# A gated feed-forward kernel: the joint stage starts at unit 3, with the x transposes and raw products of the second pass rearranged

## The chip, the cores and the metric

The kernel runs on one core of one Trainium2 chip. The metric is the device time of one execution in microseconds (us). Every time below comes from timed runs or from one profiled execution, whose trace counts from its own first instruction.

## The reference

The inputs are bfloat16: x is 2048 x 1024, w_gate and w_up are 1024 x 3584, w_down is 3584 x 1024.

```python
g = jnp.einsum("bsd,df->bsf", x, w_gate)
u = jnp.einsum("bsd,df->bsf", x, w_up)
h = gelu_tanh(g) * u
return jnp.einsum("bsf,fd->bsd", h, w_down)
```

## The kernel before

**Tiling.** The 3584 columns of the gate and up weights are cut into 14 *units* of 256. The 2048 rows of x are cut into two *passes* of 1024, each of two halves c = 0 and 1 with 512 rows. For one unit and one pass, weights (two blocks of 128 columns by two halves of the 1024 contracted elements) and x (two halves of the contraction by two halves of the rows) form a 2 x 2 by 2 x 2 block product, and the kernel forms it with seven products where the plain way takes eight. A product is four matmuls of 128 x 128 by 128 x 512, for gate and for up, so a unit and a pass take 56 matmuls. Two of the seven, the *raw products* (`raw_first`, `raw_second`, lines 229 to 236), take bfloat16 weights and x as they are. The five others take sums in float32: `s1` to `s4` of the weights (`sums_s`, line 173; `sa` is a cast), `t1` to `t4` of x (`sums_t`, line 149; `tb` is a cast).

**The separate stage.** Unit 0 of pass 0 is done in the plain way. After that `items` (line 911) lists seven pairs (unit, pass), each run by `unit` (line 252): (1,0), (2,0), (3,0), (2,1), (3,1), (1,1), (0,1). The order within `unit` is: s2·t2, s1·t1, s3·t3, s4·tb, then `whole_p4` (line 286), which calls `ahead` (raw products of later items), multiplies sa·t4 and calls `behind`. `unit` calls `aside(-2)`, `aside(-1)`, `aside(0)` and `aside(1)` at marked points, and `after_p5` behind s1·t1; there loads, transposes and GpSimd's sums are issued. Each item stores four blocks of h to DRAM (`times`, line 217).

**The joint stage.** From unit `JOINT = 4` on, a unit is done for both passes together (`joint_ops`, line 348), in an order written out by hand: `SEQUENCE_FIRST` for the first joint unit, `SEQUENCE` for the others. Here the two passes and the gate and up halves form a second 2 x 2 scheme (`inner`, line 380): seven products of two matmuls, 14, where the two passes apart take 16. It is used for s4·tb ("X") and sa·t4 ("K") in every joint unit, and for s3·t3 ("H") from unit `DIVIDED7 = 5` on. A unit of both passes takes 112 matmuls apart, 108 with X and K, 106 with all three. The inner scheme needs more sums on GpSimd: `split_b` (line 296) makes twelve 128 x 512 blocks for tb and t4 once, `split_b_rest` four more, `split_sums` (line 201) four 128 x 256 blocks for each unit and product.

**Queues.** Instructions of SyncE (which issues all DMAs), VectorE, GpSimd and TensorE go out in program order, ScalarE's too in this stage. x reaches its transposed form with DMA transposes (`transposing`, line 802), each 512 rows by 128 columns. Eight of them (pass 0, c = 1) are followed by unit 2's weights (line 827). Pass 1 needs sixteen: `XT[1, 0]` lies in `xT[1]`, `XT[1, 1]` in a tile "h01" (`late_half`, line 84) whose room t4 of pass 1 takes over later. They are issued in four groups of four (line 1071). Unit 3's weights are loaded ahead of the first group (line 1026). GpSimd makes s1 to s4 of units 2, 3, 0 and 4 and t1 to t4 of pass 1 in `at_p5` (line 925). Most tiles come from a pool of 58 slots of 2 KB in each partition; `wpool` holds two weight tiles of 8 KB.

The last stage, `down` (line 692), multiplies h with w_down in the same manner.

Of the kernel before, what the change touches and what calls it, by code (L numbers as in the profile page):

```python
# [10 lines left out]
def kernel(  # L11
# [10 lines left out]
    nc = tc.nc  # L22
# [15 lines left out]
    NKB = Dm // P  # L38
# [5 lines left out]
    NPASS = S // (2 * N)  # L44
    NU = NFB // 2
    NWARM = 7
    JOINT = 4
    DIVIDED7 = 5
    STAY = range(11, 14)
    KEEPS = [(u, n) for u in range(JOINT + 1, NU) for n in range({7: 2, 9: 2, 11: 2, 13: 3}.get(u, 1))]  # L50
    H, Q, R2 = NJ // 2, N // 2, range(2)
    SLOTS = 58
    STAGED = 3
# [27 lines left out]
    def staged():  # L81
        return opool.tile([P, N], bf16, name="o", tag="o")

    def late_half(p):
        if p:
            tile = hpool.tile([P, NJ, N], bf16, name="h01")
            XT[p, 1] = [tile[:, k] for k in range(NKB)]
        else:
            tiles = [slot([P, 2, N], bf16, "x") for _ in range(KH)]
            XT[p, 1] = [tiles[k // 2][:, k % 2] for k in range(NKB)]  # L90
# [37 lines left out]
    def load_w(u, slots=False):  # L128
        f0 = u * 2 * P
        if slots:  # L130
            w = [[slot([P, KH, 2 * P], bf16, "w") for _ in range(2)] for _ in range(2)]
        else:
            tile = wpool.tile([P, 2, NKB, 2 * P], bf16, name="w")
            w = parts(tile)
        for i, src in enumerate((w_gate, w_up)):
            src = src[:, f0 : f0 + 2 * P].rearrange("(ko ki) f -> ki ko f", ki=P)
            if slots:
                for half in range(2):
                    nc.sync.dma_start(out=w[i][half], in_=src[:, half * KH : (half + 1) * KH])
            else:  # L140
                nc.sync.dma_start(out=tile[:, i], in_=src)
        return w
# [6 lines left out]
    def sums_t(p, eng, place):  # L149
        K = range(KH)  # L150
        lo, hi = [[XT[p, c][k0 : k0 + KH] for c in range(2)] for k0 in (0, KH)]

        def put(name, k, a, b):
            t = place(name)
            eng(t, a, b, SUB)
            return t

        def put_cast(name, a):
            t = place(name)
            nc.scalar.copy(out=t, in_=a)  # L160
            return t

        return Sums(
            how={
                "t1": lambda q: [put("t1", k, lo[1][k], lo[0][k]) for k in K],
                "t2": lambda q: [put("t2", k, hi[1][k], q["t1"][k]) for k in K],
                "t3": lambda q, K=K: [put("t3", k, hi[1][k], lo[1][k]) for k in K],
                "t4": lambda q: [put("t4", k, hi[0][k], q["t2"][k]) for k in K],
                "tb": lambda q: [put_cast("tb", hi[1][k]) for k in K],
            }  # L170
        )
# [653 lines left out]
    for ko in range(NKB):  # L825
        transposing(0, 1, ko)
    ahead = load_w(2, True)

    def plain(ps, c, kos, parts=1):
        n = N // parts  # L830
# [51 lines left out]
            finish(bank[4:8], 1)  # L882
            t["t3"] = t3 + t["how"]["t3"](t, range(2, KH))

    spots = {}

    def new_room(kh, c, *names):
        tile = hpool.tile([P, H, N], f32r, name=f"h{kh}{c}")
        for i, name in enumerate(names):
            spots.setdefault(name, []).append(tile[:, i])  # L890

    new_room(0, 0, *["tb"] * KH, *["n"] * 3)
    new_room(1, 0, *["t2"] * KH, *["t1"] * 3)
    new_room(1, 1, "t1", *["t3"] * KH, *["n"] * 2)

    def place1(name):
        return spots[name].pop(0)

    def more_room():
        extra = wpool.tile([P, KH, N], f32r, name="w")  # L900
        spots["n"] += [extra[:, k] for k in range(KH)]

    def place_n():
        return spots["n"].pop(0)

    Ea, Eb, K, D = even, dd, cc, odd
    ws = {1: w, 2: ahead}
    ss = {1: s}
    sums, ns = {}, {}
    pairs = [[(2, 0), (3, 0)], [(2, 1), (3, 1)], [(1, 1), (0, 1)]]  # L910
    items = [(1, 0)] + [item for pair in pairs for item in pair]

    def loaded(u):
        return ws[u]

    def new_s(u, *names):
        if u not in ss:
            ss[u] = sums_s(loaded(u), pool)
        ss[u].make(*names)

    def raw_of(u, p, e, c):
        p1 = raw_products(e, c, p, loaded(u))
        return lambda: finish_raw(u, p, c, p1)

    def at_p5(n):
        u, p = items[n]
        if n == 0:
            pool_behind(t["t4"][-1])
            new_s(2, "s1", "s2", "s3", "s4")
        elif n == 1:  # L930
            new_s(3, "s1", "s2", "s3", "s4")
        elif n == 2:
            T[1] = sums_t(1, pool, place1)
            T[1].make("t1", "t2", "t3", "tb")
            new_room(0, 1, *["t4"] * KH, *["n"] * 3)
            T[1].make("t4")
        elif n == 3:
            new_s(0, "s1", "s2")
        elif n == 4:
            new_s(0, "s3", "s4")  # L940
            split_b("tb")
        elif n == 5:
            new_s(JOINT, "s1", "s2", "s3", "s4")
        elif n == 6:
            more_room()
            split_b("t4")

    keeps = {}
    for j, (u, n) in zip([*range(NJ)], KEEPS):
# [72 lines left out]
        if not more:  # L1022
            last_loads(what)

    turns = [(c, ko) for ko in range(NKB) for c in (1, 0)]
    loads = {(0, 0): [3], (4, 1): [JOINT]}

    def last_loads(what):
        for n in {"start": range(4, 6), "store": range(6, 10), "t4.0": range(10, 13), "s1": range(13, NJ)}.get(what, ()):
# [22 lines left out]
    with tc.manual_schedule(engines={ENG.Activation}):  # L1052
        for n, (u, p) in enumerate(items):
            first = n == 0
            m = (n - 1) // 2
            b = n % 2 == 0
            follow = pairs[m + 1] if m + 1 < len(pairs) else None

            def after_p5():
                at_p5(n)  # L1060

            def aside(part):
                if first and part < 0:
                    rest_of_0(part + 2)
                if first and part == 0:
                    t.make("t4")
                for v in loads.get((n, part), ()):
                    ws[v] = load_w(v, v == 0)
                if (n, part) == (0, 0):
                    late_half(1)  # L1070
                if (n, part) in ((0, 0), (0, 1), (1, 0), (1, 1)):
                    for c, ko in turns[:4]:
                        transposing(1, c, ko)
                    del turns[:4]

            def mid():
                if "sa" not in ss[u]:
                    ss[u]["sa"] = sums_s(loaded(u), pool)["how"]["sa"](None)

            def ahead_of_p4():  # L1080
                if b and follow:
                    raw_of(*follow[0], Ea, D)()
                    nxt["c11"] = raw_of(*follow[1], K, D)

            def behind_p4():
                if n == 2:
                    ws[0] = load_w(0, True)
                if "c11" in nxt:
                    nxt.pop("c11")()

            def after_first():
                raw_of(2, 0, even, cc)()
                nxt["c11"] = raw_of(3, 0, dd, cc)

            def p4(c12):
                times(p, 2 * u, 1, gelu(c12[0]), c12[1])
                if first:
                    whole_p4(u, p, odd, ss[u], after_first, behind_p4)
                else:
                    if n == len(items) - 1:  # L1100
                        split_b_rest("tb")
                        half_sums(JOINT, "tb", 0), half_sums(JOINT, "tb", 1)
                    whole_p4(u, p, (Ea, Eb)[b], ss[u], ahead_of_p4, behind_p4)
                    if n == len(items) - 1:
                        split_b_rest("t4")

            if first:
                banks = odd, cc, dd
                late = lambda: add(cc, nxt["p1"])
            else:  # L1110
                banks = (Eb, D, K) if b else (Ea, K, D)
                late = None
            unit(u, p, banks, ss[u], late, after_p5, aside, mid, p4)
            ss[u].pop("sa")
            if b and not first and follow:
                Ea, Eb, K, D = Ea, K, D, Eb

        E, F = [Ea, D], [K, Eb]
        last = None
        for u in range(JOINT, NU):  # L1120
            now = joint_ops(u, E, F)
            steps = SEQUENCE_FIRST if u == JOINT else SEQUENCE
            for name in steps:
                if name[0] == "@":
                    side_work(u, name[1:])
                elif name[0] != "-":
                    now[name]()
                elif last:
                    last[name]()
            last = now  # L1130
            E, F = F, E
        for name in SEQUENCE:
            if name[0] == "-":
                last[name]()
# [51 lines left out]
```

## Time and profile before

| | |
|---|---|
| median of three runs | 527.5 us (527.44 to 528.07) |
| the profiled execution's own time | 528.0 us |
| its span, first to last instruction | 526.2 us |
| TensorE (PE) busy | 521.6 us, 99% of the span, 2393 matmuls |
| VectorE (DVE) busy | 386.0 us, 73% |
| GpSimd (POOL) busy | 332.3 us, 63%; 8 tenths or more of every slice from 39 to 342 us |
| ScalarE (ACT) busy | 291.4 us, 55% |
| granted TensorE clock | 1.000 |

The timelines quoted below give the start in us, the duration in us, engine (SPq is SyncE's queue of DMA issues), line, operation, what is written and read, and the count of a merged group. Matmuls overlap in the records, so the pitch of a group is read from one group's start to the next one's.

### The profile page before, as it was taken

The numbers are of one execution on the slowest core, as the hardware profiler recorded it, in microseconds if no ns is written. First come the engines' busy times: TensorE is split into PE (matmuls) and PEld (weight loads), VectorE is DVE, ScalarE is ACT, GpSimd is POOL, SyncE is SP. The second block draws the span as 40 slices with busy tenths as digits, with TensorE's granted clock in tenths as the row PEclk, the third lists the DMA queues.
The fourth block names the chain that finished last, engine by engine and source line by source line (L and its number), as shares of the span: only waits on it lengthen the run. The fifth ranks groups of instructions, "written<-read, shape, count | busy, mean of one in ns | idle before, by whom it ended". The sixth has DMA issues, their size and how long they took to land.

```text
span 526.2 us, 7935 instructions
## 1 busy us (share of the span) xinstructions
PE 521.6 (99%) x2393; PEld 369.4 (70%) x2393; DVE 386.0 (73%) x588; ACT 291.4 (55%) x535; POOL 332.3 (63%) x339
## 2 busy tenths in 40 slices
PE   8999999999999999999999999999999999999997
PEld 5568686877667676767676676754788884488887
DVE  2984546337888889898989889896879326967934
ACT  2555755656777687868787786851135601143430
POOL 1169989988999999999999999940000000000694
PEclk9999999999999999999999999999999999999999
DMA  9685334131625357363727454999987999992732
GB/s 248 139 212 124 100 109 117 44 110 46 206 87 184 111 190 225 113 203 133 248 92 229 149 171 153 318 374 407 389 267 237 394 388 364 387 323 99 241 133 67
DMA packets 105194, 106.96 MB, mean 203 GB/s; under 512 B 19776, under 2 KB 83264, under 8 KB 105152
## 3 DMA queue, kind: packets, MB, share of 16 engines
q1 hardware_dynamic: 105152, 106.46, 62.3%
q8 instruction: 19, 0.31, 0.3%
q14 instruction: 23, 0.19, 0.1%
HBM read 73.66 MB, written 29.62 MB: 196 GB/s over the span
## 4 chain that ended last, share of the span: by engine, by line
PE 98%; DMA 1%; SPq 0%; DVE 0%; issue 0%
PE bank L120 98%; DMA w<-in_w_up_dram 1%; SPq L790 0%; SPq L810 0%; DVE st L99 0%
## 5 line engine op out<-in xcount | busy, mean ns | idle before, releaser
L120 PE MATMUL bank<-h,s 128*128 128x512 f32 x492 | 129.1, 394 | 0.0
L102 POOL TENSOR_TENSOR q<-q 128x256 fp32r<-128x256 f32 x28 | 27.0, 994 | 143.7 <-DMA q<-td 143.1
L120 PE MATMUL bank<-xT,w 128*128 128x512 bf16 (+1 forms) x472 | 107.8, 376 | 0.1
L120 PEld LDWEIGHTS bank<-h,s 128*128 128x128 f32 x492 | 92.4, 188 | 20.6
L120 PEld LDWEIGHTS <-w 128*128 128x128 bf16 x504 | 45.8, 98 | 59.0 <-issue 10.0
L102 POOL TENSOR_TENSOR s<-w 128x512 fp32r<-128x512 bf16 (+1 forms) x74 | 76.0, 1040 | 13.9 <-DMA w<-in_w_gate_dram 12.5
L120 PE MATMUL bank<-t,s 128*128 128x512 f32 x276 | 75.3, 399 | 0.0
L120 PE MATMUL bank<-q 128*128 128x512 f32 x264 | 65.6, 390 | 0.0
L120 PEld LDWEIGHTS bank<-t,s 128*128 128x128 f32 x276 | 51.9, 188 | 12.0
L116 ACT COPY p<-bank 128x512 f32<-128x512 f32 x76 | 42.9, 588 | 28.1 <-PE bank L120 28.1
L120 PEld LDWEIGHTS bank<-q 128*128 128x128 f32 x264 | 49.6, 188 | 10.4
L99 DVE TENSOR_TENSOR q<-h,h 128x512 fp32r<-128x512 bf16 x56 | 38.4, 686 | 17.1 <-DMA h<-hd 17.1
L116 ACT COPY u<-bank 128x512 f32<-128x512 f32 x62 | 35.9, 589 | 24.1 <-PE bank L120 21.5
L102 POOL TENSOR_TENSOR s<-s,s 128x256 fp32r<-128x256 f32 x57 | 42.7, 770 | 1.5
L120 PEld LDWEIGHTS <-h 128*128 128x128 bf16 x224 | 21.7, 98 | 26.5 <-issue 0.5
L102 POOL TENSOR_TENSOR s<-w,s 128x512 fp32r<-128x512 bf16 (+1 forms) x36 | 38.6, 1086 | 0.0
L99 DVE TENSOR_TENSOR xz<-bank,xz 128x512 f32<-128x512 f32 x40 | 27.6, 692 | 14.9 <-PE bank L120 8.1
L111 ACT CAST tb<-raw 128x512 fp32r<-128x512 bf16 x28 | 17.0, 631 | 36.7 <-DMA raw<-in_w_down_dram 26.1
L102 POOL TENSOR_TENSOR s<-s,w 128x512 fp32r<-128x512 f32 (+1 forms) x36 | 36.6, 1031 | 0.8
L102 POOL TENSOR_TENSOR m<-raw,m 128x512 fp32r<-128x512 bf16 x28 | 34.5, 1234 | 2.2
L99 DVE TENSOR_TENSOR bank<-bank,u 128x512 f32<-128x512 f32 x47 | 32.4, 688 | 0.0
L99 DVE TENSOR_TENSOR sum<-bank,p 128x512 f32<-128x512 f32 x14 | 9.7, 690 | 27.0 <-PE bank L120 23.1
(122 smaller groups left out, 929.6 us busy)
## 6 DMA issues: line engine op xcount, KB each, us to landing
raw<-in_w_down_dram SPq DMA_DIRECT2D x68, 256.0 KB, 3.8
q<-td SPq DMA_DIRECT2D x66, 256.0 KB, 5.4
td<-m SPq DMA_DIRECT2D x42, 256.0 KB, 2.6
hd<-o SPq DMA_DIRECT2D x72, 128.0 KB, 1.7
h<-hd SPq DMA_DIRECT2D x17, 512.0 KB, 6.9
hd<-h SPq DMA_DIRECT2D x38, 128.0 KB, 1.9
h<-hd SPq DMA_DIRECT2D x5, 768.0 KB, 8.2
out_dram<-st SPq DMA_DIRECT2D x30, 128.0 KB, 4.4
```

The source lines that it names most:

```text
L99: nc.vector.tensor_tensor(out=out, in0=a, in1=b, op=op)
L102: nc.gpsimd.tensor_tensor(out=out, in0=a, in1=b, op=op)
L111: nc.scalar.copy(out=t, in_=src)
L116: nc.scalar.copy(out=t, in_=ps)
L120: nc.tensor.matmul(ps, lhsT=lhs, rhs=rhs, start=start, stop=stop, skip_group_check=True)
```

## The change

Three things change together.

1. `JOINT` becomes 3. The items become (1,0), (2,0), (2,1), (1,1), (0,1). Unit 3 is the first joint unit (`SEQUENCE_FIRST`), unit 4 runs in `SEQUENCE`, with H still whole. Unit 3's weights go to slots and are loaded in the third item, unit 0's are not loaded again but read from the first tile. GpSimd's work is rearranged: t1 to t4 of pass 1 as eight instructions of 128 x 1024 instead of sixteen of 128 x 512, and earlier; the split of t4 after the last item has begun.
2. The sixteen transposes of pass 1 are issued in groups of 4, 4, 2, 2, 2, 2, the first behind unit 2's weights (before any store of h), the others at the points `aside(-2)`, `(-1)`, `(0)`, `(1)` of item (1,0) and `aside(-2)` of item (2,0). Their order is now: the lower half of the contraction for both c, then the upper half for c = 1, then the upper half for c = 0.
3. The raw products of (3,0) vanish from item (1,0). In item (2,0) the raw products of pass 1 are ordered: `raw_first` of unit 2, `raw_first` of unit 1, `raw_second` of unit 2, then sa·t4, then `raw_second` of unit 1 into the same banks.

```diff
-    JOINT = 4
+    JOINT = 3
+    AHEAD = {(0, -2): 4, (0, -1): 2, (0, 0): 2, (0, 1): 2, (1, -2): 2}
...
     ahead = load_w(2, True)
+    late_half(1)
+    turns = [(c, ko) for ko in range(KH) for c in (1, 0)] + [(c, ko) for c in (1, 0) for ko in range(KH, NKB)]
+
+    def turn_some(n):
+        for c, ko in turns[:n]:
+            transposing(1, c, ko)
+        del turns[:n]
+
+    turn_some(4)
...
-    items = [(1, 0)] + [item for pair in pairs for item in pair]
+    items = [(1, 0), (2, 0), (2, 1), (1, 1), (0, 1)]
...
+    def two_sums(name, a, b):
+        T[1][name] = spots[name]
+        for k in (0, 2):
+            i = slice(k, k + 2)
+            pool(twos[name, k], a[:, i], twos[b, k] if isinstance(b, str) else b[:, i], SUB)
...
             new_s(2, "s1", "s2", "s3", "s4")
+            T[1] = {}
+            two_sums("t1", XL[:, :KH], xT[1][:, :KH])
...
         elif n == 3:
-            new_s(0, "s1", "s2")
+            split_b("tb")
+            new_s(JOINT, "s1", "s2")
         elif n == 4:
-            new_s(0, "s3", "s4")
-            split_b("tb")
-        elif n == 5:
-            new_s(JOINT, "s1", "s2", "s3", "s4")
-        elif n == 6:
-            more_room()
-            split_b("t4")
+            new_s(JOINT, "s3", "s4")
+            half_sums(JOINT, "tb", 0), half_sums(JOINT, "tb", 1)
...
-    loads = {(0, 0): [3], (4, 1): [JOINT]}
+    loads = {(2, 1): [3]}
...
+                turn_some(AHEAD.get((n, part), 0))
+                if (n, part) == (1, -2):
+                    two_sums("t2", XL[:, KH:], "t1")
+                    two_sums("t3", XL[:, KH:], XL[:, :KH])
...
             def ahead_of_p4():
-                if b and follow:
-                    raw_of(*follow[0], Ea, D)()
-                    nxt["c11"] = raw_of(*follow[1], K, D)
+                if n == 0:
+                    raw_of(2, 0, even, cc)()
+                elif n == 1:
+                    p1 = [raw_first(e, 1, loaded(v)) for e, v in ((Eb, 2), (D, 1))]
+                    raw_second(K, 1, loaded(2))
+                    finish_raw(2, 1, K, p1[0])
+
+                    T[1]["tb"] = spots["tb"]
+                    for k in range(KH):
+                        nc.scalar.copy(out=spots["tb"][k], in_=XT[1, 1][KH + k])
+                    new_room(0, 1, *["t4"] * KH, *["n"] * 3)
+                    two_sums("t4", xT[1][:, KH:], "t2")
+                    new_s(0, "s1", "s2", "s3", "s4")
+
+                    def second_half():
+                        raw_second(K, 1, loaded(1))
+                        finish_raw(1, 1, K, p1[1])
+
+                    nxt["c11"] = second_half
+                elif n == 3:
+                    raw_of(0, 1, Ea, D)()
...
             def p4(c12):
...
+                if n == len(items) - 1:
+                    split_b_rest("tb")
+                    more_room()
+                    split_b("t4")
+                whole_p4(u, p, banks[0], ss[u], ahead_of_p4, behind_p4)
+                if n == len(items) - 1:
+                    split_b_rest("t4")
```

## The prediction

> **What bounds the kernel now.** I read the page first (busy time, then the chain that ended last), then the waits of TensorE, then its timeline over the first 140 us, and last the timelines of SyncE and GpSimd over the stretch that changes.
>
> ```profile
> PE 521.6 (99%) x2393; PEld 369.4 (70%) x2393; DVE 386.0 (73%) x588; ACT 291.4 (55%) x535; POOL 332.3 (63%) x339
> ...
> PE 98%; DMA 1%; SPq 0%; DVE 0%; issue 0%
> ```
>
> ```profile
> PE bank L855 <- PEq L1170: 0.8, 1, 0.8
> PE bank L797 <- DMA xn<-in_x_dram: 0.5, 1, 0.5
> ```
>
> TensorE is busy 99% of the span, and its two waits both fall before the first real product. So the time is the sum of the matmuls: taking a matmul out gains exactly its pitch, and any new wait of TensorE is lost in full, for nothing later is idle to absorb it.
>
> ```profile
> 32.09 7.08 PE L120 MATMUL bank<-xT,w 128*128 128x512 bf16 x32
> 38.82 2.19 PE L120 MATMUL bank<-t,sa 128*128 128x512 f32 x8
> 40.85 5.60 PE L120 MATMUL bank<-t,s 128*128 128x512 f32 x24
> 46.29 1.98 PE L120 MATMUL bank<-tb,s 128*128 128x512 f32 x8
> 48.10 1.98 PE L120 MATMUL bank<-t,sa 128*128 128x512 f32 x8
> ...
> 109.15 3.63 PE L120 MATMUL bank<-xT,w 128*128 128x512 bf16 x16
> ```
>
> These rows give the pitches. The 32 float32 matmuls from 40.85 to 48.10 take 7.25 us, 0.2266 us each. From 32.09 to 40.85 lie 32 bfloat16 and 8 float32 ones: 8.76 - 1.81 = 6.95 us, 0.217 us each. The joint stage starts at 109.15.
>
> **Step 1: the matmuls.** Unit 3 takes 112 matmuls with its passes apart and 108 together: X and K fall from 16 to 14 each, all float32. Units 1, 2 and 0 stay, and unit 4 keeps its 108 in the other sequence. That is 4 x 0.2266 = **0.91 us less**. No other change touches the number of matmuls, so this is all there is to gain.
>
> **Step 2: when TensorE needs the transposed x of pass 1.** Item (2,0) began at 40.85. Item (1,0) loses the 16 raw matmuls of (3,0), 3.47 us, so it begins at 37.38. Its 32 float32 matmuls end at 44.63. Then come the two `raw_first`, 16 bfloat16 matmuls, to 48.10. `raw_second` of unit 2 reads the upper half for c = 0, one transposed block per matmul: at 48.10, 48.32, 48.53 and **48.75**. The last two blocks are the last two transposes in the new order.
>
> **Step 3: when those transposes are issued.** SyncE's rows of before:
>
> ```profile
> 23.64 3.86 SPq L223 DMA_DIRECT2D hd<-h  x4
> 27.59 0.39 SPq L141 DMA_DIRECT2D w<-in_w_gate_dram  x1
> 28.03 0.67 SPq L141 DMA_DIRECT2D w<-in_w_up_dram  x1
> 28.75 2.26 SPq L804 DMA_TRANSPOSE h<-in_x_dram  x1
> 31.05 1.26 SPq L804 DMA_TRANSPOSE xT<-in_x_dram  x1
> 32.35 1.26 SPq L804 DMA_TRANSPOSE h<-in_x_dram  x1
> 33.66 1.26 SPq L804 DMA_TRANSPOSE xT<-in_x_dram  x1
> 35.02 1.00 SPq L223 DMA_DIRECT2D hd<-h  x2
> 36.07 1.12 SPq L804 DMA_TRANSPOSE h<-in_x_dram  x1
> ...
> 47.02 1.26 SPq L804 DMA_TRANSPOSE xT<-in_x_dram  x1
> 48.37 1.30 SPq L223 DMA_DIRECT2D hd<-h  x1
> ```
>
> ```profile
> L804 SPq DMA_TRANSPOSE h<-in_x_dram x8: 1122/1258/2262, 28.7 to 52.2; - x8
> L804 SPq DMA_TRANSPOSE xT<-in_x_dram x8: 1252/1258/1266, 31.1 to 53.5; - x8
> ...
> DMA to landing us min/median/max: 2.6/2.8/5.7
> ```
>
> A transpose holds SyncE for 1.30 us from start to start (31.05, 32.35, 33.66), the first behind a store for 1.17. Two stores take 1.1. The first transpose behind a load of 1 MB of weights took 2.30 (28.75 to 31.05). A block lands 2.8 us after its issue begins (the second fence is the answer for line 804: minimum, median and maximum in ns of an issue, then the landing).
>
> After the change SyncE is free at 23.6, where the first store of h now stands, right behind unit 2's 1 MB. From there it has sixteen transposes and nine stores, and never waits for a store's data: the products of item (1,0) are all made by about 39 us. In order: four transposes, the first slow, 6.2 us, to 29.8; two stores to 30.9; four transposes, 5.1 us, to 36.0; two stores to 37.1; two groups of two, 5.1, to 42.2; two stores to 43.3; two transposes, 2.5, to 45.8; three stores, 1.6, to 47.4. The last two transposes are issued at 47.4 and 48.6, and at 2.8 us each would land at 50.2 and 51.4, after the need at 48.53 and 48.75.
>
> One thing comes on top. The transpose issued at 47.02 in before was late:
>
> ```profile
> q8 instruction: 1, 0.02, 5.2%
> issues: line engine op xcount, KB each, median us to landing
> xT<-in_x_dram SPq DMA_TRANSPOSE x1, 3.7
> ```
>
> In the window 47 to 48.3 there is a fetch of instructions (queue q8), the transpose took 3.7 us to land, and the store behind it held SyncE for 1.30 us instead of about 0.5. TensorE has executed the same number of matmuls at 48.1 in both kernels (16 fewer raw ones, then 16 more), so if the fetch follows TensorE's program, it falls on the last two transposes. That makes 51.1 for the first of them and up to 52.4 for the last. I take 52.0 for the last block, between 51.4 and 52.4: TensorE waits **52.0 - 48.75 = 3.25 us**, most of it before the third matmul, the rest before the fourth. The bounds: with the first transpose at the common 1.30 and no fetch, issue at 47.6, landing at 50.4, a wait of 1.6; with both, 52.4 and 3.7.
>
> **Step 4: GpSimd and the sums.**
>
> ```profile
> 39.95 2.30 POOL L102 TENSOR_TENSOR s<-w 128x512 fp32r<-128x512 bf16 x2
> ...
> 49.00 4.57 POOL L102 TENSOR_TENSOR h<-h,xT 128x512 fp32r<-128x512 bf16 x4
> ...
> 112.26 2.55 POOL L102 TENSOR_TENSOR h<-h 128x512 fp32r<-128x512 f32 x2
> 114.76 0.68 POOL L102 TENSOR_TENSOR s<-w 128x256 fp32r<-128x256 bf16 x1
> ```
>
> At 39.95 unit 2's sums are made; until 49.00 unit 3's followed, eight in 9.05 us, now t1 does. The 128 x 1024 form is not in the trace; it does twice the work of the 1.14 us form, so between 2 x 1.0 and 2 x 1.3 us (the float32 form, 2.55 for two), and I take 2.27. Then t1 is ready at 44.5, t2 at 49.0, t3 at 53.6. Item (2,1) starts at 53.4 plus the wait, so needs t2 at 56.6, t1 at 58.4 and t3 at 60.2. t4 must wait until ScalarE's four casts of tb have read "h01":
>
> ```profile
> 54.27 2.18 ACT L160 CAST h<-h 128x512 fp32r<-128x512 bf16 x4
> ```
>
> They take 2.2 us and stand behind the gelu of the late raw products (about 53.7), so t4 starts at 56.0, is made at 60.5 and needed at 63.9. Unit 0's sums end at 69.6, needed at 78. Then the split of tb (six at 1.3 us), unit 3's sums, its four tb parts, the rest of tb, the split and rest of t4 and four t4 parts (7.9 + 9.1 + 2.9 + 2.6 + 7.9 + 2.6 + 2.7) end at 105.3. One unit of both passes fewer (32 x 0.217 + 80 x 0.2266 = 25.07) puts the joint stage at 84.1, 87.3 with the wait; its first K product that needs the t4 parts comes 32 bfloat16 and 64 float32 matmuls later, at 108.7. That is 3.4 us of cover, 2.6 if TensorE had not waited (t4 then starts at 53.6). This costs nothing, but it is the thinnest cover of GpSimd; each us lost beyond it would be lost in the end.
>
> **Step 5: the reused banks.** `raw_second` of unit 1 writes the banks of unit 2's, whose sum and product VectorE must have read.
>
> ```profile
> 40.09 0.69 DVE L99 TENSOR_TENSOR h<-g,bank 128x512 bf16<-128x512 f32 x1
> ```
>
> This row is the same chain for (3,0): its raw matmuls ended at 39.0, the last read of its banks at 40.8, 1.8 us later. In the new order 8 float32 matmuls (1.81 us) and four bfloat16 ones for the first bank (0.87) lie between, 2.7 us, so it is covered by 0.9 us; without that cover it would cost at most 1.8. Fewer loads (unit 0's weights) shorten nothing, because no wait of TensorE hangs on them.
>
> **The sum.** -0.91 + 3.25 = +2.3 us: 528.0 becomes 530.3 for a profiled execution, whose own time lies 0.5 above the median of the runs; from the median of 527.5 it is **529.8 us**.
>
> **The rivals.**
>
> - *The transposes are in time* (the other side). If the last one were issued by about 45.9, TensorE would not wait, and the time would be 527.5 - 0.9 = 526.6. The point from which it decides is a landing at 48.7; SyncE would have to save 2.7 us over 25 transposes and stores. Against it: no transpose of pass 1 took less than 1.12 us, and behind another none less than 1.25. For it: only that SyncE is seen here behind other loads than it will be. Chance 0.08.
> - *A short wait*: no slow first transpose and no fetch in the way, 1.6 us of wait, 527.5 - 0.9 + 1.6 = 528.2 (527.3 to 528.5). Against it, both slow rows. Chance 0.14.
> - *A second loss*: after the wait TensorE's clock falls, or GpSimd loses more than its 3.4 us to full slots. The row for the clock:
>
> ```profile
> 0.78 3.15 PE L855 MATMUL bank<-const-bfloat16-1.0 128*128 128x512 bf16 x7 [0.78 <-PEq L1170]
> ```
>
>   The seven first matmuls, after idle time, took 3.15 us where seven at 0.217 take 1.5: 1.6 us lost. Paid again, 529.8 + 1.6 = 531.4. Against it: the wait is broken by a matmul. Chance 0.16. The Trainium skill, "TensorE: Matmul & The Clock Gate", Part 1: The HAM clock gate, says that the array drops to half clock after a window of about 3.4 us without work; by it a broken wait of 3.25 us just escapes, and no run here shows one of that length.
> - *The saving is not there*: unit 4 in `SEQUENCE` stalls, because H whole comes where the divided form left room. Against it: X, K and G stand alike in both sequences and fewer copies are asked of ScalarE. It would add to the forecast, and is counted in the case before.
>
> **How the numbers follow.** Forecast, a wait of 2.3 to 3.8 us, 528.9 to 530.4: chance 0.62. A measurement of this kernel can tell about 0.2%, 1.06 us, from no change. The first rival gives 0.17% less, so faster by over 0.2% only with luck: 0.03 of its 0.08. Within: its other 0.05 and 0.13 of the short wait, 0.18. Slower: 0.62 + 0.16 + 0.01 of the short wait, 0.79. The range leaves out the first rival below and half of the second loss above: 527.3 to 531.6.
>
> **What would show it.** Right: TensorE's timeline has a gap of about 3 us in the 8 bfloat16 matmuls that start at 48.1, released by a DMA into xT; SyncE's last transposes are issued near 47.4 and 48.6; no other gap up to the end; the joint stage starts near 87. Wrong: the last block lands before 48.7 and the chain has no gap; a wait for GpSimd in the first K products; or bfloat16 matmuls of 0.42 us behind the gap.

## The result, and the profile after

| | before | after |
|---|---|---|
| median of 20 runs | 528.0 us (527.43 to 528.96) | 529.57 us (528.18 to 533.74) |
| ratio of after to before, 95% interval | | 1.0038 [1.0024, 1.0052] |
| the profiled execution's own time | 528.0 us | 528.45 us |
| its span | 526.2 us | 526.7 us |
| granted TensorE clock in it | 1.000 | 1.000 |

The change makes the kernel slower by 0.4%. The profiled execution shows a smaller loss, 0.45 us, than the median does, 1.6 us; what the traces tell of this comes below.

The first and the fourth part of the page of after, busy time and the chain that ended last:

```profile
PE 520.9 (99%) x2389; PEld 367.9 (70%) x2389; DVE 390.6 (74%) x598; ACT 293.9 (56%) x542; POOL 337.5 (64%) x339
...
PE 91%; SPq 3%; DVE 2%; DMA 2%; issue 1%; ACT 0%; DVEq 0%
```

Four matmuls are gone, as the change says. But the chain, which was TensorE for 98% of the span, now leaves TensorE and goes back through SyncE's queue. The waits of TensorE in after (total us, times, longest) say where:

```profile
PE bank L124 <- DMA xT<-in_x_dram: 1.0, 1, 1.0
PE bank L868 <- PEq L1189: 0.8, 1, 0.8
PE bank L801 <- DMA xn<-in_x_dram: 0.7, 1, 0.7
```

The last two were there before. The first is new. TensorE's timeline of after places it:

```profile
37.43 5.60 PE L124 MATMUL bank<-t,s 128*128 128x512 f32 x24
42.87 1.97 PE L124 MATMUL bank<-tb,s 128*128 128x512 f32 x8
44.68 4.39 PE L124 MATMUL bank<-xT,w 128*128 128x512 bf16 x19
50.11 1.24 PE L124 MATMUL bank<-xT,w 128*128 128x512 bf16 x5 [1.03 <-DMA xT<-in_x_dram]
51.00 2.20 PE L124 MATMUL bank<-t,sa 128*128 128x512 f32 x8
...
85.52 3.63 PE L124 MATMUL bank<-xT,w 128*128 128x512 bf16 x16
```

Nineteen bfloat16 matmuls at 0.217 us take 4.12 us, and from 44.68 to 50.11 lie 5.43: 1.3 us are lost (the row counts 1.03, because it lets each matmul end later than its pitch). The gap is inside the second raw product of unit 2, three matmuls in, and its releaser is a transposed block of x. Nothing else is lost up to the end: -0.91 + 1.3 = +0.4, and the span grew by 0.5.

SyncE's rows of after around the sixteen transposes:

```profile
23.09 1.18 SPq L808 DMA_TRANSPOSE h<-in_x_dram  x1
24.31 1.26 SPq L808 DMA_TRANSPOSE xT<-in_x_dram  x1
...
41.71 2.43 SPq L808 DMA_TRANSPOSE xT<-in_x_dram  x2
44.25 1.89 SPq L227 DMA_DIRECT2D hd<-h  x3
46.18 2.43 SPq L808 DMA_TRANSPOSE xT<-in_x_dram  x2
48.71 8.70 SPq L227 DMA_DIRECT2D hd<-h  x5
```

Three things differ from the forecast. SyncE was free at 23.09, 0.5 us earlier than assumed. The first transpose behind unit 2's weights held it from 23.09 to 24.31, no longer than any other. And the last two were issued at 46.18 and 47.36, so 1.2 us earlier than foreseen. The share of the instruction queue and the landings of the transposes in after, first of the window 40 to 46:

```profile
q8 instruction: 1, 0.02, 1.0%
...
xT<-in_x_dram SPq DMA_TRANSPOSE x2, 3.8
```

and of the window 46 to 52, where no instruction queue is listed:

```profile
xT<-in_x_dram SPq DMA_TRANSPOSE x2, 2.6
```

The fetch fell on the two transposes before the last two. Those took 3.8 us (median) to land, and TensorE did not wait for them. But SyncE is in order, and the first of the three stores behind them held it for 0.91 us where 0.52 is usual; so the fetch pushed the last two back by 0.4 us. Those took 2.6 us, and the very last landed at 50.07.

The median over the runs is another matter. Of the 20 runs of after, 14 have a granted clock of 1.000 and lie from 528.18 to 530.01 with a median of 529.22. Five have 0.996 or 0.997 and lie from 530.89 to 531.52, and one has 0.949 (533.74). The runs of before that list a clock are all at 0.999 or 1.000. One execution outside this table, of `e2_c0_first`, took 586.57 us at a clock of 0.852 and is in no ratio. So the loss is not the same in each run, and in a quarter of them something like 2 us comes on top together with a lower clock. The profiled execution was one of the quickest. Two traces from further down, `e5_second_later` and `e7_raw_undone`, tell why the wait is usually longer: their queue is the same up to the last two transposes, but there the fetch comes up to 1.5 us earlier, beside the issue of a transpose, and that issue takes 2.70 and 2.29 us instead of 1.25. In e5:

```profile
41.12 3.88 SPq L808 DMA_TRANSPOSE xT<-in_x_dram  x2
...
46.64 2.43 SPq L808 DMA_TRANSPOSE xT<-in_x_dram  x2
```

The last two are issued 24.1 us behind the first transpose of pass 1 in both, and 23.1 us behind it in the profiled execution of after (in e7 a third of a microsecond of this comes from a slower transpose near 24). With 1.0 us more, its wait would be about 2.3 us (an estimate from these rows).

### The profile page after: what moved, and what is told of

It reads as the page before. It is cut to its first block, busy times and chain, and to the rows that moved or that the text cites. A ratio compares the mean times of both kernels' runs of the same rounds, so it can differ in the third digit from the quotient of the medians.

```text
span 526.7 us, 7917 instructions
## 1 busy us (share of the span) xinstructions
PE 520.9 (99%) x2389; PEld 367.9 (70%) x2389; DVE 390.6 (74%) x598; ACT 293.9 (56%) x542; POOL 337.5 (64%) x339
## 4 chain that ended last, share of the span: by engine, by line
PE 91%; SPq 3%; DVE 2%; DMA 2%; issue 1%; ACT 0%; DVEq 0%
PE bank L124 91%; SPq L808 2%; DMA xT<-in_x_dram 1%; DVE t L103 1%; DMA w<-in_w_up_dram 1%; DVE s L103 1%; SPq L227 0%; DVE h L103 0%; SPq L794 0%; ACT g L218 0%; DVE sum L103 0%; SPq L814 0%; DVE st L103 0%; DVE bank L103 0%; DVEq L103 0%
## 5 line engine op out<-in xcount | busy, mean ns | idle before, releaser
L124 PE MATMUL bank<-h,s 128*128 128x512 f32 x500 | 132.6, 395 | 0.0
L124 PE MATMUL bank<-xT,w 128*128 128x512 bf16 (+1 forms) x472 | 109.0, 377 | 1.1 <-DMA xT<-in_x_dram 1.0
L124 PEld LDWEIGHTS bank<-h,s 128*128 128x128 f32 x500 | 93.9, 188 | 21.1
L106 POOL TENSOR_TENSOR s<-w 128x512 fp32r<-128x512 bf16 (+1 forms) x76 | 77.8, 1039 | 11.0 <-DMA w<-in_w_gate_dram 11.0
L124 PE MATMUL bank<-t,s 128*128 128x512 f32 x276 | 76.5, 400 | 0.0
L120 ACT COPY p<-bank 128x512 f32<-128x512 f32 x72 | 40.7, 589 | 30.7 <-PE bank L124 26.8
L124 PEld LDWEIGHTS bank<-q 128*128 128x128 f32 x264 | 49.6, 188 | 10.4
L106 POOL TENSOR_TENSOR s<-s,s 128x256 fp32r<-128x256 f32 x60 | 44.8, 770 | 1.6
L103 DVE TENSOR_TENSOR xz<-bank,xz 128x512 f32<-128x512 f32 x44 | 30.2, 691 | 18.5 <-PE bank L124 14.3
L103 DVE TENSOR_TENSOR bank<-bank,u 128x512 f32<-128x512 f32 x49 | 33.7, 688 | 0.0
L103 DVE TENSOR_TENSOR v<-bank,v 128x512 f32<-128x512 f32 x44 | 29.2, 684 | 2.1 <-PE bank L124 1.7
```

The lines of the kernel that those rows point to most:

```text
L103: nc.vector.tensor_tensor(out=out, in0=a, in1=b, op=op)
L106: nc.gpsimd.tensor_tensor(out=out, in0=a, in1=b, op=op)
L120: nc.scalar.copy(out=t, in_=ps)
L124: nc.tensor.matmul(ps, lhsT=lhs, rhs=rhs, start=start, stop=stop, skip_group_check=True)
```

## The experiments

The theory: TensorE waits for the last two transposed blocks of pass 1, whose place in SyncE's queue is too late for `raw_second` of unit 2, and -0.91 us plus this wait is the whole change. The rivals: the other sequence of the joint stage or GpSimd's rearranged sums cost something too, or the saving is not there. Each ratio is to the kernel before, timed beside it on the same chip.

**The reader later, the queue as it is.** `e5_second_later` moves both `raw_second` one product later, unit 2's behind sa·t4 of (2,0), unit 1's behind s2·t2 of (2,1); the transposes and stores keep their places.

```diff
+                if (n, part) == (2, 0):
+                    raw_second(K, 1, loaded(1))
...
-                    raw_second(K, 1, loaded(2))
-                    finish_raw(2, 1, K, p1[0])
+                    nxt["p1_11"] = p1[1]
...
-                        raw_second(K, 1, loaded(1))
-                        finish_raw(1, 1, K, p1[1])
+                        raw_second(K, 1, loaded(2))
+                        finish_raw(2, 1, K, p1[0])
...
+            finish_raw(1, 1, K, nxt.pop("p1_11"))
```

> The changed kernel with the raw products that read the upper half for c = 0 moved later on TensorE: raw_second of unit 2 behind the sa.t4 of item (2,0) instead of ahead of it, raw_second of unit 1 behind the s2.t2 of item (2,1). The transposes stay as they are. Theory (the whole loss is TensorE's wait for the last blocks): the need moves from 48.1 - 48.75 to 49.9 - 50.6, so 1.8 us of the wait go: no wait in a profile like that of the changed kernel, 527.1 to 527.8, granted clock 1.000 in every run, runs within 1.5 us. Rival (a part of the loss lies in the later stages): it stays above 528.3.

Measured: 527.41 us (526.59 to 527.67), ratio 0.999 [0.9981, 0.9999], clock 1.000 in all eleven runs. TensorE's timeline:

```profile
47.30 2.19 PE L124 MATMUL bank<-t,sa 128*128 128x512 f32 x8
49.34 0.82 PE L124 MATMUL bank<-xT,w 128*128 128x512 bf16 x3
50.57 1.24 PE L124 MATMUL bank<-xT,w 128*128 128x512 bf16 x5 [0.42 <-DMA xT<-in_x_dram]
```

Eight float32 matmuls (1.8 us) now stand ahead of the reader, and 0.42 us of wait are left by the row, 0.6 by the pitch. Against after, 2.2 us are won by the medians, with no transfer touched. So the wait is the loss, and the saving is there.

**The reader sooner.** `e7_raw_undone` undoes one piece of the reordering of the raw products and nothing else: `raw_second` of unit 2 goes directly behind its `raw_first`, 1.74 us earlier.

```diff
-                    p1 = [raw_first(e, 1, loaded(v)) for e, v in ((Eb, 2), (D, 1))]
+                    first2 = raw_first(Eb, 1, loaded(2))
                     raw_second(K, 1, loaded(2))
-                    finish_raw(2, 1, K, p1[0])
+                    finish_raw(2, 1, K, first2)
+                    p1 = [None, raw_first(D, 1, loaded(1))]
```

> The changed kernel with the reordering of the raw products undone in part: raw_second of unit 2 directly behind its raw_first, raw_first of unit 1 after it. The upper half for c = 0 is read 1.73 us earlier, from 46.4 on. Theory: the wait grows by just that, 529.6 + 1.7 = 531.3, with more runs in which the clock falls. Rival (the order of the raw products matters by their banks or copies, not by the transposes): 529 to 530.

Measured: 531.5 us (531.44 to 532.67), ratio 1.007 [1.0058, 1.0082]; the clock is 0.997 in four of five runs. TensorE's timeline:

```profile
47.15 0.38 PE L124 MATMUL bank<-xT,w 128*128 128x512 bf16 x1 [0.29 <-DMA xT<-in_x_dram]
49.52 0.38 PE L124 MATMUL bank<-xT,w 128*128 128x512 bf16 x1 [2.00 <-DMA xT<-in_x_dram]
50.93 4.65 PE L124 MATMUL bank<-xT,w 128*128 128x512 bf16 x13 [1.04 <-DMA xT<-in_x_dram]
55.23 2.19 PE L124 MATMUL bank<-t,sa 128*128 128x512 f32 x8
```

The wait grows to 3.3 us, in three pieces with single matmuls between. And the 13 matmuls behind it take 4.30 us instead of 2.82: seven of them stand 427 ns apart, half speed. So this piece of the reordering is a gain, of about 1.9 us with the clock in it; without it the change would cost 0.7%.

**The transposes later.** `e6_late_in_order` puts the last four at `aside(1)` of item (2,0), behind all stores of (1,0) and one more, in the order of the change. `e3_late_reversed` does the same with those four in reverse order, so that the first block needed lands last.

```diff
-    AHEAD = {(0, -2): 4, (0, -1): 2, (0, 0): 2, (0, 1): 2, (1, -2): 2}
+    AHEAD = {(0, -2): 4, (0, -1): 2, (0, 0): 2, (1, 1): 4}
...
+    turns = [...] + [(0, ko) for ko in reversed(range(KH, NKB))]     # e3 only
```

> As the run with the last four transposes late and reversed (one wait of 4.0 us, then 0.43 us for a matmul), but in order: the same four issues, so the last block lands at the same time, but TensorE waits in pieces of about 0.4, 1.0, 1.0 and 1.0 us with a matmul between. If only an unbroken wait halves the clock: 527.1 + 3.3 = 530.4, clock 1.000. If the sum of the idle time counts: 532.5, clock 0.996 as there.

> The changed kernel with the last four transposes moved behind the first store of item (2,0), and in reversed order, so that the block which raw_second reads first lands last. Theory of the wait: it lands near 51.7, one unbroken wait of 3.6 us from 48.1: 527.1 + 3.6 = 530.7 with the clock at 1.000. With the theory that a long unbroken wait halves the clock for some 3.5 us (as in the runs of the changed kernel with a granted clock of 0.996 and 531.5 us): 532.5 in most runs, a granted clock of 0.996, and bfloat16 or float32 matmuls of 0.43 us behind the gap in the trace.

Measured: in order 530.92 us (529.37 to 531.85), ratio 1.0051 [1.0035, 1.0066]; reversed 532.75 us (531.55 to 533.53), ratio 1.0091 [1.0078, 1.0105]. The two waits, first in order and then reversed:

```profile
48.41 0.38 PE L124 MATMUL bank<-xT,w 128*128 128x512 bf16 x1 [0.38 <-DMA xT<-in_x_dram]
49.74 0.38 PE L124 MATMUL bank<-xT,w 128*128 128x512 bf16 x1 [0.95 <-DMA xT<-in_x_dram]
50.98 1.24 PE L124 MATMUL bank<-xT,w 128*128 128x512 bf16 x5 [0.86 <-DMA xT<-in_x_dram]
51.86 2.19 PE L124 MATMUL bank<-t,sa 128*128 128x512 f32 x8
```

```profile
51.83 3.57 PE L124 MATMUL bank<-xT,w 128*128 128x512 bf16 x8 [3.96 <-DMA xT<-in_x_dram]
54.84 3.44 PE L124 MATMUL bank<-t,sa 128*128 128x512 f32 x8
58.12 1.90 PE L124 MATMUL bank<-xT,w 128*128 128x512 bf16 x8
```

In order, 2.2 us of wait in three pieces by the rows, and full speed behind them: the eight float32 matmuls from 51.86 to the next group at 53.89 take 2.03 us, in after 2.05. Reversed, one wait of 4 us, and half speed behind it: those eight take 3.28, and all sixteen matmuls from 51.83 to 58.12 take 6.3 us instead of 3.6. The clock of the runs agrees: 0.994 to 0.997 in every run reversed, 1.000 in the profiled run in order (529.37). But three of the six runs in order, 531.15 to 531.85, show 0.997 too. So whether a wait in short pieces drops the clock is decided run by run; what the traces show of this stands in the next section, under the rivals.

**The transposes earlier.** `e1_early` issues twelve in a row behind unit 2's first four; `e8_two_groups` issues eight in a row at `aside(-1)`.

```diff
+    AHEAD = {(0, -2): 12}                  # e1_early
+    AHEAD = {(0, -2): 4, (0, -1): 8}       # e8_two_groups
```

> The changed kernel with its last twelve transposes in one group at aside(-2) of item (1,0) instead of groups of 4, 2, 2, 2, 2; only SyncE's order differs. Theory (TensorE waits for the last two transposes of pass 1; nothing else is lost): the last one is issued near 43 and lands near 46, before 48.7, so no wait is left, the time is 528.0 - 0.9 = 527.1 (ratio 0.998), the runs scatter by 1.5 us as before's do, and the granted clock is 1.000 in every run. Rival (the loss lies with GpSimd or in the joint stage): it stays near 529.6 and the scatter stays at 5 us.

> The changed kernel with eight transposes behind the two stores of unit 0's second half, in place of four groups of two; the five stores of item (1,0) and of the raw products of (2,0) go out behind them, near 46 to 48. In the run with all twelve ahead of all stores ScalarE waited 13.1 us for a slot that a store of h still held, and TensorE 10.4 us for ScalarE. If those first two stores are the ones whose slots are needed: no wait for slots, the last block lands near 47.4, 527.1 and clock 1.000. If any later store holds a slot that is needed: ScalarE or VectorE wait again, and TensorE with them, 530 to 536.

Measured: 538.74 us (537.64 to 539.44), ratio 1.0204 [1.019, 1.0219], and 533.59 us (533.33 to 534.45), ratio 1.0109 [1.0095, 1.0122]. Both lose far more than the wait that they were to remove. ScalarE, SyncE and TensorE of `e1_early`:

```profile
47.55 0.59 ACT L120 COPY p<-bank 128x512 f32<-128x512 f32 x1 [13.13 <-DMA hd<-h]
```

```profile
40.25 5.17 SPq L808 DMA_TRANSPOSE xT<-in_x_dram  x4
45.52 22.19 SPq L227 DMA_DIRECT2D hd<-h  x12
```

```profile
48.28 6.38 PE L124 MATMUL bank<-t,s 128*128 128x512 f32 x20 [10.43 <-ACT p L120]
```

Read from the last row back: TensorE waits 10.4 us for ScalarE's copy of a bank; the copy waits 13.1 us for a store of h (`hd<-h`); the store stands behind twelve transposes and is issued at 45.52. The copy doesn't read h. It needs a slot of the pool, and the block of h holds it until its store has landed. In `e8_two_groups` it is a later store's slot, with `raw_first` of unit 1 waiting: ScalarE's cast of `sa` waits for the slot, the gelu behind it on ScalarE comes late, VectorE's product of h waits for the gelu, and VectorE's sum behind that frees the bank.

```profile
51.29 5.21 PE L124 MATMUL bank<-xT,w 128*128 128x512 bf16 x16 [4.77 <-DVE sum L103]
```

```profile
ACT sa L115 <- DMA hd<-h: 6.4, 1, 6.4
DVE h L103 <- ACT g L218: 6.2, 1, 6.2
```

So the stores between the groups are not idle fill: they free the slots in which the next results are put.

**The early transposes alone.** Before, with the sixteen transposes of after and nothing else of the change (`JOINT` stays 4). In `e4_transposes_only` unit 3's load stays at `aside(0)`, in `e9_transposes_only` it moves ahead.

```diff
-    loads = {(0, 0): [3], (4, 1): [JOINT]}
+    loads = {(0, -2): [3], (4, 1): [JOINT]}     # e9 only
...
-                if (n, part) in ((0, 0), (0, 1), (1, 0), (1, 1)):
...
+                turn_some(AHEAD.get((n, part), 0))
```

> The kernel before (joint stage from unit 4) with the transposes of pass 1 in the groups and the order of the changed kernel. Its raw products of pass 1 come at 57, long after the last landing near 51, so the theory expects no difference: 528.0 within 0.3. Rival (transposes ahead of the stores of h cost by themselves, in slots or DMA time): 528.5 to 530.

> The kernel before (joint stage from unit 4, raw products as they were) with the transposes of pass 1 in the changed kernel's groups and order. In the earlier run of this kind unit 3's weights stayed at aside(0), behind ten transposes, and TensorE waited 7.1 us for them; here they are loaded at aside(-2), behind four. Theory: the raw products of pass 1 come at 57, the last block lands near 52, nothing waits: 528.0 within 0.4. Rival (transposes between the stores cost by themselves, in slots or in DMA time): 528.8 or more.

Measured: 537.71 us (536.67 to 537.9), ratio 1.0183 [1.017, 1.0197], and 533.03 us (532.32 to 533.82), ratio 1.0101 [1.0086, 1.0117]. The first tells nothing of the question: the load of unit 3 itself came too late behind the transposes.

```profile
42.16 6.56 PE L121 MATMUL bank<-xT,w 128*128 128x512 bf16 x16 [7.07 <-DMA w<-in_w_gate_dram]
```

The second refutes what I expected. Its waits in the window 25 to 60:

```profile
DVE sum L100 <- DMA hd<-h: 5.0, 1, 5.0
ACT p L117 <- DMA hd<-h: 4.8, 1, 4.8
POOL s L103 <- DMA hd<-h: 4.7, 1, 4.7
...
PE bank L121 <- DVE sum L100: 3.5, 1, 3.5
```

Three engines wait for slots held by stores, TensorE 3.5 us behind them. But this run doesn't hold the transposes alone either. The chain leads back from TensorE to the pair of stores at 37.20, which were issued at 34.47 in after, and from there through these rows:

```profile
30.00 0.40 SPq L142 DMA_DIRECT2D w<-in_w_gate_dram  x1
30.45 0.65 SPq L142 DMA_DIRECT2D w<-in_w_up_dram  x1
31.15 2.05 SPq L805 DMA_TRANSPOSE h<-in_x_dram  x1
```

Unit 3's load takes 1.15 us of SyncE, and the transpose behind it 0.9 more than in after (1.12 at that place), so 2.1 of the 2.7 us come from the moved load. What the early transposes would cost with no load among them was not run. With (3,0) still among the items, unit 3's raw results want slots in the same stretch too; after has no such wait, but how much of that is due to (3,0) is not shown.

**The other order of c.** `e2_c0_first` issues the upper half for c = 0 ahead of c = 1.

```diff
-    turns = [...] + [(c, ko) for c in (1, 0) for ko in range(KH, NKB)]
+    turns = [...] + [(c, ko) for c in (0, 1) for ko in range(KH, NKB)]
```

> The changed kernel with the same groups, but the upper half for c = 0 ahead of that for c = 1. Theory: TensorE's raw products have their blocks by 42, and GpSimd's t2 gets its last block near 50 instead of 42, which its cover takes: 527.1 to 527.7, clock 1.000. Rival (any late block is paid in full, whoever reads it): GpSimd ends 3 us later, and TensorE waits for t3 or t4 of item (2,1): 528.5 to 530.

Measured: median 529.03 us, ratio 1.0023 [1.0014, 1.0033]. The wait for xT is gone and another is there, in TensorE's waits:

```profile
PE bank L124 <- POOL s L106: 0.6, 1, 0.6
...
PE bank L124 <- POOL h L106: 0.5, 1, 0.5
```

and in GpSimd's own, from 44 to 66 us:

```profile
POOL h L106 <- DMA h<-in_x_dram: 4.9, 2, 3.5
```

GpSimd's t2 and t3 read the upper half for c = 1, which is now last; its t4 ends at 61.2 instead of 58.4, too late for sa·t4 of (2,1), which waits 0.45 us. GpSimd is then still 2.7 us behind when it makes the weights' sums for the joint stage (one of them at 105.74 instead of 103.00), and TensorE's other wait, 0.6 us, is for such a sum, between 110 and 150 us. The late block still costs, through GpSimd: two short waits, 1.1 us. The result lies between the two theories.

**The best of both.** With e5's order of the raw products, the last two transposes go ahead of one store of (1,0) in `e10_one_store_behind`, ahead of three in `e11_three_stores_behind`.

```diff
-    AHEAD = {(0, -2): 4, (0, -1): 2, (0, 0): 2, (0, 1): 2, (1, -2): 2}
+    AHEAD = {(0, -2): 4, (0, -1): 2, (0, 0): 2, (0, 1): 2}      # e10
+                if n == 0:                                      # e10, in behind_p4
+                    turn_some(2)
+    AHEAD = {(0, -2): 4, (0, -1): 2, (0, 0): 2, (0, 1): 4}      # e11
```

> The version with raw_second later (527.4, a wait of 0.4 us left for the last block, landing at 50.5) with its last two transposes one store earlier: ahead of the store of the last product of item (1,0) instead of behind it. The last block lands 0.5 us earlier: the wait goes, 527.0. If that store's slot is needed within its 2.5 us of delay, VectorE, ScalarE or GpSimd wait for it, and it is 527.4 to 530.

> As the version with raw_second later, with its last four transposes in one group at aside(1) of item (1,0), ahead of three stores. The last block lands 1.5 us earlier, near 49, and no wait for it is left in any run: 527.0, at most 527.6. But the three stores land near 50 instead of 47 to 48; if one of their slots is needed by then, an engine waits as in the two runs with long groups, and it is 528 to 531.

Measured: 527.12 us (526.26 to 527.79), ratio 0.9987 [0.9979, 0.9996], and 527.26 us (526.46 to 528.33), ratio 0.9991 [0.9982, 1.0]. Neither has a wait for xT. `e10_one_store_behind` beats both kernels: it gets 0.8 of the 0.91 us that the four matmuls are worth. Its SyncE:

```profile
42.18 3.40 SPq L808 DMA_TRANSPOSE xT<-in_x_dram  x2
45.67 1.00 SPq L227 DMA_DIRECT2D hd<-h  x2
46.72 2.43 SPq L808 DMA_TRANSPOSE xT<-in_x_dram  x2
```

The last two are issued at 46.72, half a microsecond later than in after. It is the reader's new place that makes them early enough. That the one store less ahead of them helps is not shown: in this trace TensorE reaches the reader at 50.31, in e5's at 49.34, and the intervals of e5, e10 and e11 lie almost on each other.

## Why the prediction was right, point by point

The direction and the range held, and 529.8 lies 0.2 us above the median of 529.57. That closeness is luck: three errors nearly cancel. The prediction started from the median of three runs, 527.5, where twenty runs have 528.0; it took the wait for 1.1 us longer than a usual run seems to have it; and it left out the runs with the lower clock, which lift the median by 0.35 us (529.57 against 529.22). Its change was +2.3 us, the medians differ by 1.6, and the ratio gives +2.0 [+1.3, +2.8].

- **Step 1, the matmuls: right.** With the wait gone, e10 is 0.8 us below before; with 0.6 us of it left, e5 is 0.4 below.
- **Step 2, the need: right.** The third matmul of `raw_second` would have started at 44.68 + 18 x 0.217 = 48.6, the forecast was 48.53; the third was 0.1 us late and the fourth 1.2. The forecast had most of the wait before the third.
- **Step 3, the wait: right in kind, and the term that was mis-sized.** 3.25 us were forecast, at least 1.6; the profiled execution lost 1.3. Its pieces: SyncE was free 0.5 us earlier, the first transpose was 1.1 us shorter, the store beside the fetch 0.4 longer, and the last block took 0.7 us less to land, together 1.9 us less.
  *The first transpose behind 1 MB of weights is slow*: 2.30 us were taken, 1.22 measured (23.09 to 24.31). The row of before belongs to unit 3's load, which is issued as two DMAs; behind it the transpose is slow again in e9 (2.05) and e4 (2.43). Unit 2's load is issued as four, and behind it the first transpose took 1.18 to 1.19 us in all twelve traces that have it there. In six of these the second took 1.6 to 1.8 instead of 1.26. Why is open.
  *The fetch of instructions falls on the last two*: it fell on the two before, so the last landed 2.7 us after its issue and not 3.4. The premise holds and the conclusion does not. In all ten kernels with unit 3 in the joint stage the fetch starts when TensorE has started 207 to 214 matmuls, also in e1, where it stood still for 10.4 us before and the fetch came at 54.6; so it does follow TensorE's program. But in before, e4 and e9 that count is 231 to 234. The change moved the place by some 20 matmuls; by which rule stays open. And the fetch does delay the last two by way of SyncE's queue, by 0.4 us here and by 1.0 to 1.4 in e5 and e7, a path that the forecast left out.
  Over the runs the size comes closer: the 14 runs at clock 1.000 have a median of 529.22, 2.1 us above e10's 527.12, so about 2 us of wait in a usual run, which agrees with the estimate of 2.3 from e5's and e7's queue. None of those runs was profiled but the one.
- **Step 4, GpSimd: right.** Three of its rows in after:

```profile
39.81 4.30 POOL L106 TENSOR_TENSOR h<-h,xT 128x1024 fp32r<-128x1024 bf16 x2
...
54.14 4.28 POOL L106 TENSOR_TENSOR h<-xT,h 128x1024 fp32r<-128x1024 bf16 x2 [1.62 <-issue]
...
102.36 0.67 POOL L106 TENSOR_TENSOR s<-w,s 128x256 fp32r<-128x256 bf16 x1
```

  The 128 x 1024 form took 2.15 us, not 2.27. t4 did have to wait, and was made at 58.4 (60.5 foreseen). The t4 parts are made at 103.0, 4.3 us ahead of the K product that reads them, which TensorE starts at 107.27 without a wait. The cover that was thinner in effect is that of t4 of pass 1 and of what GpSimd makes after it: 2.8 us more were enough for the two waits of e2.
- **Step 5, the reused banks: right.** TensorE has no wait for VectorE.
- **The joint stage** starts at 85.5, not 87.3: the difference of 1.8 us is the wait that was forecast too long (3.25 - 1.3 = 1.9).
- **The rivals.** *In time* needs the reader moved, as e5 and e10 do. *A short wait* describes the profiled execution: 1.3 us. *A second loss* had 0.16 and names what five runs in 20 show: the clock. A stretch at half speed costs 1.5 us in e7 (4.30 instead of 2.82), which is 0.3% of the span, and 0.997 is the clock that such a run reports. That the runs of after at 0.996 and 0.997 have the same half-speed stretch is inferred from this; none of them was profiled. The sixth, 0.949 at 533.74, does not fit it: at half speed that clock would stand for some 54 us and a loss near 27 (an estimate), and what happened there is open.

  The clock records of the traces say more. The stretches at 0.5 last 3.41 us in e7 (51.61 to 55.02), e8 and e9, 6.83 in e3 (50.69 to 57.52) and 10.24 in e1 and e4. Each begins a whole number of times 3.41 us behind the moment at which that trace records the first rise to full clock, which differs by run: 3.8 us in e7, 6.3 in e3. In the 3.41 us just before the fall TensorE was busy for 1.04 us in e7, 0.58 in e3, and not at all in e8 and e9. Counted in the same steps, the stretches that hold the waits have 2.51 and 2.10 us of work in e6 and 2.37 in after, and there the clock stayed. So, as far as these traces show, what counts is the work in a window of 3.41 us whose edges lie differently in each run. That explains how a wait in pieces can cost the clock in one run and not in the next; that it is what happened in the three slower runs of e6 and the five of after is inferred. The Trainium skill, "TensorE: Matmul & The Clock Gate", Part 1: The HAM clock gate, describes activity counted in a free-running window of about 3.4 us and a drop to half clock after an idle one. The traces agree with the length and with the run-dependent phase; in e7 the window before the fall was not idle but 31% busy.
- **The saving is not there**: refuted by e5, e10 and e11.
- **Not foreseen at all**: how many things hang on the stores. The prediction priced a store as 0.5 us of SyncE. That what stands ahead of stores holds slots, and costs 5 to 11 us (e9, where it is a load and transposes, e8 and e1), was in no step; in after it happened to cost nothing.
- **What would show it**: a gap of about 3 us and a joint stage near 87 were named for right; the profiled execution has 1.3 and 85.5. Bfloat16 matmuls of 0.42 us behind the gap were named for wrong; that trace has none, the quarter of the runs with the lower clock probably do.

## What to carry to other kernels

When a step is moved ahead on the engine that sets the time, follow each in-order queue down to the last item that the step reads, and compare landing with need: here the last of sixteen transposes was 1.3 us late in the profiled run, and about 2 in a usual one. Where an item is late, first search for independent work to put ahead of its reader (e5: 2.2 us won by moving matmuls alone); crowding the queue costs more, because what is pushed back there may be what frees the buffers (e1: 11 us lost). And a wait of TensorE costs more than its length once the clock falls behind it, in some runs and not in others, so time such a kernel often: one profile can show the mild case.

## What the runs showed of the hardware

- Behind a wait of 4.0 us TensorE ran at 427 ns for a 512-column matmul, half speed, until the granted clock rose again at 57.5 us (e3: 2.7 us lost), and also behind waits of 0.29, 2.00 and 1.04 us with single matmuls between (e7: 1.5 us lost). Behind 0.38, 0.95 and 0.86 us it did not in the profiled run (e6).
- The granted clock fell and rose on steps of 3.41 us whose phase differs by run (e1, e3, e4, e7, e8, e9). It fell behind steps with 0 to 1.04 us of TensorE work and stayed up with 2.10 us or more (e6, after).
- One fetch of instructions on the DMA engines came with a landing of 3.8 us for the two transposes beside it, instead of 2.6 (after), or with an issue of 2.3 to 2.7 us instead of 1.25 (e5, e7). It came at 207 to 214 matmuls in all ten kernels with unit 3 in the joint stage, wherever in time that was.
- A transpose directly behind a 1 MB load in two DMAs held SyncE for 2.05 to 2.43 us (before, e9, e4); behind the same size in four DMAs for 1.18 (after).
